# Retention and a routed expert layer on one core: the first job's second weights are loaded behind its rows, two lists are set a step apart, and the rows of zeros go out in three scatters

## The chip, the cores and the metric

The kernel runs on one core of a Trainium2 chip. The metric is the device time of one execution in microseconds (us). Several executions of the kernel before were timed, and one execution was also taken by the hardware profiler. Engines are named as the profile names them: PE (matrix multiplies; PEld is its weight load), DVE and ACT (element work), POOL (element work, and the issue of indirect transfers), SP (the issue of plain transfers).

## The reference, cut to what matters

```python
# q, k, v: (B=4, H=8, S=768, D=64)
gamma = 1.0 - 2.0 ** (-5.0 - np.arange(H))
for t in range(S):
    state = gamma * state + k[:, :, t] outer v[:, :, t]
    y[:, :, t] = (q[:, :, t] @ state) / sqrt(D)

x = y as 3072 tokens of 512 features
logits = x @ w_gate + modality_bias[modality_id]      # 8 experts
e_idx = argmax(logits);  gate_w = softmax(logits)[e_idx]
for e in range(8):
    rows = x[e_idx == e]
    out[e_idx == e] = gate_w * (relu(rows @ w1[e]) @ w2[e])   # w1: 512x1024, w2: 1024x512
```

A decayed linear attention gives one row for each of 3072 tokens. Each row then goes to one of eight experts, a two-layer network, and the result goes back to the token's place.

## The kernel before, in words

**Attention and routing.** The 3072 tokens are 24 chunks of 128. `retention` works through them, by `whole_*` functions for the first nine chunks and by `quarters` for the rest; it is a generator that yields several times a chunk. Every three chunks are a group (eight groups, numbered from 0), and `route(gr)` routes one. Its pieces are small functions on a list `todo`: `a` and `a1` find each token's expert, `b` ranks tokens and 256-row candidates (PE tiles `pc` and `rk`), `c` scatters the three chunks' rows to `x_dram`, sorted by expert (POOL, L485), and makes the one-hot `ohs` (PE tile `pk` ahead of it), and `d` writes an event list `lst` (PE tile `pt`). `wait` does nothing; it takes one place. `tick` runs the next piece: at each yield of `retention` before the first job, and at every second step of a job later. Such lists follow groups 1, 2, 4, 5 and 6. Each names two full slots of 256 rows that can be computed already; so there are ten event jobs (two for each list, tags e10, e11, e20 and so on) and two jobs from the final list. Two units of 32 rows, and a loop for what is left over, take the rest.

**A job** loads its rows (`xg0`, `xg1`, SP, L810) and its expert's weights as raw f32 (`raw1i` for w1 and `raw2i` for w2, 512 KB each, L778, or L780 where the load is skipped if the wanted expert is there already). Each raw tile is cut in a high part (`hi`, ACT, L784) and a low part (`lo`, DVE, L786). The rows are transposed on PE, eight matmuls (`flip_x`, tile `xp`, L829). Then `first_slot` computes h (L844) and `second` computes o (L859), three products each; the result is scattered to the output by POOL (L872). During a job, every third step does a piece of the next chunk of attention.

**The guess.** After group 0 the most frequent expert is guessed to be that of the first job, and `everything` loads its w1 and w2 (L778) before the list is known. When the list of group 1 is there, the job starts: its rows and then both weights again, conditionally. After that, `ahead` counts the remaining yields down from AHEAD = 6: the first two pieces of w1 are cut at 4 and 3, the rows are flipped at 2, and the job begins at 0.

**Padding.** Each expert's last slot is filled with rows of zeros: `pad_a` and `pad_b` compute, for each of eight experts, 256 row numbers (11 DVE operations), and `pad_c` issues two scatters for an expert (POOL, L545) of 128 rows each, most of whose numbers are out of range. The zeros are a tile of 128 x 514 that POOL fills at L173. The rows of the first job from the final list wait for all of them.

**What sets the order.** PE, ACT, DVE and SP run in the order in which the Python calls emit their instructions; POOL's order is set by a scheduler. A new tile in a pool's buffer waits for the readers of the old one. Attention's `kq` tiles are in a pool of four buffers, with the exception of four early ones that lie in tiles of the jobs.

## Time and profile before

| | us |
|---|---|
| median of 3 executions | 432.29 |
| their lowest and highest | 431.11, 435.65 |
| the profiled execution | 429.24 |
| span in the profile | 427.2 |
| PE busy | 403.8 (95%) |
| DVE busy | 247.5 (58%) |
| ACT busy | 207.7 (49%) |
| POOL busy | 103.1 (24%) |

A row of the timeline gives the start, the duration, the engine, the line, the operation with its output and inputs, how many instructions are merged, and in brackets how long the engine stood idle before and what ended that. PEclk is the TensorE clock that was granted, 1.00 being full speed. "issue" is a time in which the engine waited for nothing that the profile shows.

### The profile page before, as it was taken

To read this page: it belongs to the slowest core of one execution; us is meant where nothing else is said; L and a number is where in the kernel's file an instruction comes from. 1 tells how busy PE (TensorE), PEld (TensorE's weight loads), DVE (VectorE), ACT (ScalarE), POOL (GpSimd) and SP (SyncE) were. 2 spreads that over 40 slices of the span, in tenths; PEclk is the share of its full clock that TensorE was granted. 3 is DMA by queue.
4 is the path that set the end of the run, shared out by engine and by line. 5 is a ranking of instruction groups with operands and counts; after the bars stand their busy time and mean duration, and the time that the engine had idled before them with its cause. 6 is when DMAs were issued, how large, how long until landed. Compare 5 with 4: busy or idle time off the path is not lost.

```text
span 427.2 us, 12026 instructions
## 1 busy us (share of the span) xinstructions
PE 403.8 (95%) x4596; PEld 352.8 (83%) x4596; DVE 247.5 (58%) x590; ACT 207.7 (49%) x420; POOL 103.1 (24%) x130
## 2 busy tenths in 40 slices
PE   4998869999999999999999999999999999999994
PEld 3887749988968977988898998989899898967863
DVE  1775537855726674756754765768565574634700
ACT  1233346754627444655645564655465563636511
POOL 2424401233033114112510210130486100002001
PEclk9998979999999999999999999999999999999998
DMA  8999748877787955137760213762253898999001
GB/s 289 398 405 371 270 143 263 297 265 252 255 294 261 302 209 187 50 125 254 241 224 28 94 58 123 269 201 76 67 174 130 310 337 280 383 387 345 27 0 45
DMA packets 30891, 92.79 MB, mean 217 GB/s; under 512 B 5550, under 2 KB 5678, under 8 KB 30832
## 3 DMA queue, kind: packets, MB, share of 16 engines
q1 hardware_dynamic: 25360, 77.83, 52.8%
q0 software_dynamic: 5184, 13.67, 8.6%
q8 instruction: 37, 0.61, 0.6%
q10 hardware_dynamic: 288, 0.50, 0.3%
q14 instruction: 22, 0.18, 0.1%
HBM read 94.84 MB, written 17.21 MB: 262 GB/s over the span
## 4 chain that ended last, share of the span: by engine, by line
PE 54%; issue 17%; DMA 5%; DVE 3%; POOL 3%; ACT 2%; POOLq 1%; SPq 0%; ACTq 0%
PE o_e L859 20%; PE h_e L844 20%; PE x L379 4%; PE st L267 3%; PE sc L267 3%; PE y L267 2%; DVE lo_e L786 2%; PE xp_e L829 2%; ACT hi_e L784 1%; DMA kv<-in_qkv_dram 1%; POOL out_dram L872 1%; POOL x_dram L545 1%; DMA x_dram<-zer,pad_i 1%; DMA xg_e<-x_dram 1%; DMA wa_u<-in_w_dram 1%
## 5 line engine op out<-in xcount | busy, mean ns | idle before, releaser
L786 DVE TENSOR_TENSOR lo_e<-raw,hi_e 128x1024 fp32r<-128x1024 f32 x80 | 99.8, 1248 | 83.9 <-ACT hi_e L784 75.9
L844 PE MATMUL h_e<-xTh,hi_e 128*128 128x256 f32 x320 | 91.8, 287 | 0.0
L844 PE MATMUL h_e<-xTl,hi_e 128*128 128x256 f32 x320 | 90.3, 282 | 0.0
L844 PE MATMUL h_e<-xTh,lo_e 128*128 128x256 f32 x320 | 90.3, 282 | 0.0
L784 ACT CAST hi_e<-raw 128x1024 fp32r<-128x1024 f32 x80 | 83.7, 1047 | 3.9 <-DMA raw<-in_w_dram 3.9
L859 PE MATMUL o_e<-hi_e,hTh 128*128 128x512 f32 x160 | 66.3, 414 | 0.0
L859 PE MATMUL o_e<-lo_e,hTh 128*128 128x512 f32 x160 | 63.1, 395 | 0.0
L859 PE MATMUL o_e<-hi_e,hTl 128*128 128x512 f32 x160 | 63.1, 394 | 0.0
L844 PEld LDWEIGHTS h_e<-xTh,hi_e 128*128 128x128 f32 x320 | 60.7, 190 | 0.7
L844 PEld LDWEIGHTS h_e<-xTh,lo_e 128*128 128x128 f32 x320 | 60.6, 190 | 0.3
L844 PEld LDWEIGHTS h_e<-xTl,hi_e 128*128 128x128 f32 x320 | 60.7, 190 | 0.0
L1032 POOL TENSOR_TENSOR vd<-kv,cst 128x512 f32<-128x512 f32 x24 | 27.2, 1133 | 96.7 <-PE y L267 38.7
L793 ACT ACTIVATE hTh<-h_e 128x256 fp32r<-128x256 f32 x80 | 30.7, 386 | 34.0 <-PE h_e L844 29.9
L872 POOL DMA_INDIRECT out_dram<-o_e,xg_e x20 | 20.6, 1032 | 110.2 <-ACT o_e L871 90.4
L401 ACT ACTIVATE xs<-x,cst 128x64 f32<-128x64 f32 x96 | 22.2, 314 | 43.7 <-DVE lh L387 25.1
L794 DVE SCALAR_TENSOR_TENSOR hTl<-h_e,hTh 128x256 fp32r<-128x256 f32 x80 | 33.1, 419 | 16.5 <-ACT hTh L793 14.8
L485 POOL DMA_INDIRECT x_dram<-xs,pos x24 | 26.9, 1119 | 44.9 <-DVE a L212 17.2
L859 PEld LDWEIGHTS o_e<-lo_e,hTh 128*128 128x128 f32 x160 | 30.1, 188 | 7.1
L859 PEld LDWEIGHTS o_e<-hi_e,hTh 128*128 128x128 f32 x160 | 30.1, 188 | 6.1
L859 PEld LDWEIGHTS o_e<-hi_e,hTl 128*128 128x128 f32 x160 | 30.2, 189 | 5.5
L871 ACT ACTIVATE o_e<-o_e,xg_e 128x512 f32<-128x512 f32 x20 | 13.8, 690 | 40.8 <-issue 23.9
L379 PE MATMUL x<-wgt,yT 128*128 128x144 f32 x192 | 30.7, 304 | 1.8 <-issue 1.8
(193 smaller groups left out, 677.8 us busy)
## 6 DMA issues: line engine op xcount, KB each, us to landing
raw<-in_w_dram SPq DMA_DIRECT2D x104, 512.0 KB
kv<-in_qkv_dram SPq DMA_DIRECT2D x24, 512.0 KB
kq<-in_qkv_dram SPq DMA_DIRECT2D x23, 512.0 KB
xg_e<-x_dram SPq DMA_DIRECT2D x20, 257.0 KB
wa_u<-in_w_dram SPq DMA_DIRECT2D x8, 512.0 KB
wb_u<-in_w_dram SPq DMA_DIRECT2D x16, 256.0 KB
xg_s<-x_dram SPq DMA_DIRECT2D x4, 257.0 KB
x_dram<-xs,pos POOLq DMA_INDIRECT x24
```

The source lines that it names most:

```text
L267: nc.tensor.matmul(out_, l, r, start=start, stop=True, skip_group_check=True)
L379: nc.tensor.matmul(px[:, g], yT[:, 2 * u + g], wgt[:, 2 * u + g], start=(g == 0), stop=(g == 1), skip_group_check=True,)
L401: nc.scalar.activation(x[:, i], px[:, i // 2, rows(i % 2)], AF.Copy, scale=gain[:, c, 4 * u + i : 4 * u + i + 1],)
L485: ins = nc.gpsimd.indirect_dma_start(out=x_dram[:, :], out_offset=bass.IndirectOffsetOnAxis(ap=pos[:, i : i + 1], axis=0), in_=xs, in_offs ...
L784: nc.scalar.copy(hi, raws[m][i])
L786: nc.vector.tensor_tensor(lo, raws[m][i], hi.bitcast(F32), op=ALU.subtract)
L793: nc.scalar.activation(hi, src, AF.Relu)
L794: nc.vector.scalar_tensor_tensor(lo, src, 0.0, hi.bitcast(F32), op0=ALU.max, op1=ALU.subtract)
L844: nc.tensor.matmul(ph, s["w1"][f // 2][wi][:, o : o + P], s["xT"][kc // 2][a][:, kc % 2, :], start=(n == 0), stop=(n == 3 * KC - 1),)
L859: nc.tensor.matmul(po, hT[f][a][:, hh * P : (hh + 1) * P], s["w2"][f // 2][wi][:, (f % 2) * DM : (f % 2 + 1) * DM], start=(n == 0), stop=( ...
L872: ins = nc.gpsimd.indirect_dma_start(out=out[:, :], out_offset=bass.IndirectOffsetOnAxis(ap=xg.bitcast(I32)[:, DM : DM + 1], axis=0), in_= ...
L1032: ins = nc.gpsimd.tensor_tensor(vds[n], vv, by[:, n % NCH].unsqueeze(2).to_broadcast([P, H, D]), op=ALU.mult)
```

## The change

1. The guess loads w1 alone. The first job loads its w2 without a condition, behind its rows and the conditional w1.
2. AHEAD is 5, the flip stands at `ahead == 1`, and the first list's pieces are `a1, wait, b, c, d`: b, c and d come one step later. The cuts and the beginning of the job stay at their steps, since the count starts one step later.
3. The fifth group's pieces (gr 4) are `a, a1, wait, b, c, d, rows_out`, one step later from b on.
4. Both row registers of the first job are read ahead of its first row load.
5. The four `kq` buffers become slices of one tile `four`, which the padding fills with zeros for runs of eight rows (128 x 4112), and which also holds the last units' w1.
6. The padding is three scatters: two of runs of eight rows, one of single rows. Their row numbers take 26 DVE operations in place of 11, three small matmuls in place of one, and two more places on `todo` ahead of the scatters.

```diff
@@ constants @@
+RUN = 8
-AHEAD = 6
+AHEAD = 5
@@ buffers of kq @@
+    four = ld.tile([P, max(4 * QW, RUN * ROW)], F32, name="four", bufs=1)
+    fours = [four[:, i * QW : (i + 1) * QW] for i in range(4)]
+    free = [i for i in range(NN) if ("kq", i) not in lent]
+        if kind == "kq":
+            return fours[free.index(n) % 4].rearrange("p (a b) -> p a b", a=2)
@@ pad_m, pad_b, pad_c (new) @@
+        for i in range(3):
+            nc.tensor.matmul(
+                tot[:, i : i + 1], spread[:, i], ones[:, 0:1], start=True, stop=True
+            )
+        mid["zero"] = zer = four[:, : RUN * ROW].rearrange("p (r c) -> p r c", c=ROW)
+        nc.gpsimd.memset(zer, 0.0)
...
+    def pad_c(i):
+        n = RUN if i else 1
+        zer = mid["zero"].rearrange("p r c -> p (r c)")
+        ins = nc.gpsimd.indirect_dma_start(
+            out=x_dram[:, :].rearrange("(n r) c -> n (r c)", r=n),
+            out_offset=bass.IndirectOffsetOnAxis(ap=mid["pad"][:, i : i + 1], axis=0),
+            in_=zer[:, : n * ROW],
+            in_offset=None,
+            bounds_check=ZROW // n - 1,
+            oob_is_err=False,
+        )
@@ load_rows, unit, start_job @@
-            r = r() if callable(r) else r
-        wa = [ld.tile([P, QW], F32, tag="kq", name=f"wa{i}_{tag}", bufs=4) for i in range(4)]
+        wa = fours
-        s["at"] = [lambda h=h: reg(lst, at + h * n + i, EMPTY) for h in range(s["nh"])]
+        s["at"] = [reg(lst, at + h * n + i, EMPTY) for h in range(s["nh"])]
@@ route @@
-            todo.extend([a1, b, c, d])
+            todo.extend([a1, wait, b, c, d])
-            todo.extend([a, a1, b, c])
+            todo.extend([a, a1, wait, b, c])
-                todo.extend([wait, final_m, wait, final_b, pad_a, wait, pad_b, wait])
-                todo.extend([lambda e=e: pad_c(e) for e in range(NE)])
+                todo.extend([wait, final_m, wait, final_b, pad_a, wait, pad_m, wait, pad_b, wait])
+                todo.extend([lambda i=i: pad_c(i) for i in (1, 2, 0)])
@@ everything @@
                 raw(guess, 1)
-                raw(guess, 2)
                     raw(job, 1, guess)
-                    raw(job, 2, guess)
+                    raw(job, 2)
-                if ahead == 2:
+                if ahead == 1:
                     flip_x(job)
```

How this moves the instructions is shown at three places. On SP, before, this stands between the guess's last raw tile and the first job's rows (`lst_798` is the first list in memory; each read of it gives one register, `xg_e_803` and `xg_e_815` are the two halves of the rows):

```order
L778 DMA raw_109<-in_w_dram 128x1024
L111 DMA kv_739<-in_qkv_dram 128x1024
L958 TENSOR_LOAD lst_798
L958 ISA x2
L810 ISA
L810 DMA xg_e_803<-x_dram 128x514
L958 TENSOR_LOAD lst_798
L958 ISA x2
L810 ISA
L810 DMA xg_e_815<-x_dram 128x514
L958 TENSOR_LOAD lst_798
L958 ISA x2
```

And now, from the guess's last raw tile on (the tiles' numbers differ):

```order
L807 DMA raw_105<-in_w_dram 128x1024
L120 DMA kv_702<-in_qkv_dram 128x1024
L986 TENSOR_LOAD lst_810
L986 ISA x2
L986 TENSOR_LOAD lst_810
L986 ISA x2
L838 ISA
L838 DMA xg_e_835<-x_dram 128x514
L838 ISA
L838 DMA xg_e_837<-x_dram 128x514
L986 TENSOR_LOAD lst_810
L986 ISA x2
```

The four raw tiles 106 to 109 (w2) no longer stand ahead of `kv`, and both row registers are read ahead of the first row load. The w2 loads now come behind the conditional w1, which ends with `raw_105`:

```order
L809 DMA raw_105<-in_w_dram 128x1024
L807 ISA
L807 DMA raw_106<-in_w_dram 128x1024
L807 ISA
L807 DMA raw_107<-in_w_dram 128x1024
L807 ISA
L807 DMA raw_108<-in_w_dram 128x1024
L807 ISA
L807 DMA raw_109<-in_w_dram 128x1024
L120 DMA kv_867<-in_qkv_dram 128x1024
L114 DMA four<-in_qkv_dram 128x1024
```

They stand ahead of the next chunks' kv and kq (a slice of `four`), where the four conditional w2 loads stood.

On PE, before, the flip (`xp`) stands behind the last matmuls of chunk 8's y and ahead of the work on chunk 9 (`st`, `y` with input `s_9`):

```order
L319 MATMUL y_8_944<-a_773,vd_701 64x128 x4
L319 MATMUL y_8_945<-a_773,vd_701 64x128 x4
L829 MATMUL xp_e_969<-cst,xg_e_803 128x128
L829 MATMUL xp_e_969<-cst,xg_e_815 128x128
L829 MATMUL xp_e_969<-cst,xg_e_803 128x128
L829 MATMUL xp_e_969<-cst,xg_e_815 128x128
L829 MATMUL xp_e_978<-cst,xg_e_803 128x128
L829 MATMUL xp_e_978<-cst,xg_e_815 128x128
L829 MATMUL xp_e_978<-cst,xg_e_803 128x128
L829 MATMUL xp_e_978<-cst,xg_e_815 128x128
L267 MATMUL st_897<-vd_866,kv_320 64x64 x2
L267 MATMUL y_987<-kq_287,s_9_906 64x64 x2
```

And now:

```order
L276 MATMUL sc_958<-four 64x64 x2
L276 MATMUL y_957<-four,s_9_927 64x64 x2
L276 MATMUL sc_958<-four 64x64 x2
L276 MATMUL y_957<-four,s_9_927 64x64 x2
L857 MATMUL xp_e_993<-cst,xg_e_835 128x128
L857 MATMUL xp_e_993<-cst,xg_e_837 128x128
L857 MATMUL xp_e_993<-cst,xg_e_835 128x128
L857 MATMUL xp_e_993<-cst,xg_e_837 128x128
L857 MATMUL xp_e_1002<-cst,xg_e_835 128x128
L857 MATMUL xp_e_1002<-cst,xg_e_837 128x128
L857 MATMUL xp_e_1002<-cst,xg_e_835 128x128
L857 MATMUL xp_e_1002<-cst,xg_e_837 128x128
```

The flip has gone behind the first half of chunk 9's small matmuls; between `y_8` and the flip there are now 32 of them. In the same list, `pc` and `rk` of the first list's `b` have gone behind chunk 8's scores (`sc_8`, L277, 16 matmuls), `pk` behind the routing product of chunk 6 (`x`, L379), and `pt` behind chunk 7's y; on DVE the operations from `gt` to `ohs` have gone behind chunk 8's `a`.

On PE in the fifth group, before, the pieces of `b` (`pc`, `rk`) stand inside the first output half of job e20 (`o_e_2584`), behind its first 12 matmuls:

```order
L859 MATMUL o_e_2584<-hi_e_2374,hTl_2392 128x512
L859 MATMUL o_e_2584<-lo_e_2376,hTh_2391 128x512
L619 LDWEIGHTS crep
L619 MATMUL pc_2609<-ones,crep 96x1
L456 LDWEIGHTS upper
L456 MATMUL rk_2618<-oh_2541,upper 128x24
L457 LDWEIGHTS ones
L457 MATMUL rk_2618<-ebase,ones 128x24
L463 LDWEIGHTS ones
L463 MATMUL rk_2618<-cnt_95,ones 128x24
L463 LDWEIGHTS ones
L463 MATMUL rk_2618<-oh_2541,ones 128x16
```

And now:

```order
L887 MATMUL o_e_2565<-hi_e_2497,hTl_2515 128x512
L887 MATMUL o_e_2565<-lo_e_2499,hTh_2514 128x512
L648 LDWEIGHTS crep
L648 MATMUL pc_2671<-ones,crep 96x1
L465 LDWEIGHTS upper
L465 MATMUL rk_2680<-oh_2522,upper 128x24
L466 LDWEIGHTS ones
L466 MATMUL rk_2680<-ebase,ones 128x24
L472 LDWEIGHTS ones
L472 MATMUL rk_2680<-cnt_95,ones 128x24
L472 LDWEIGHTS ones
L472 MATMUL rk_2680<-oh_2522,ones 128x16
```

They stand behind the end of that half, ahead of the second half `o_e_2696`. In the same way `pk` has gone behind the first 12 matmuls of the second half, and `pt` behind its end.

More of the change, by code (lines that the diff above doesn't have):

```diff
@@ L497, in pad_a @@
     def pad_a():
-        tot = bank("tot")[:, :NE]
-        nc.tensor.matmul(tot, ones, cnt[NGRP], start=True, stop=True)
-        shape = [P, NE, 2]
-        at = cp.tile(shape, F32, name="pad_at")
-        row = cp.tile([P, 2], F32, name="pad_row")
-        nc.gpsimd.iota(
-            row, [[P, 2]], base=0, channel_multiplier=1, allow_small_or_imprecise_dtypes=True
-        )
-        num = cp.tile([P, NE], F32, name="pad_num")
-        nc.vector.tensor_copy(num, tot)
-        numi = cp.tile([P, NE], I32, name="pad_numi")
@@ L543, in pad_c @@
-    def pad_c(e):
-        for h in range(2):
-            ins = nc.gpsimd.indirect_dma_start(
-                out=x_dram[:, :],
-                out_offset=bass.IndirectOffsetOnAxis(ap=mid["pad"][:, e, h : h + 1], axis=0),
-                in_=mid["zero"],
-                in_offset=None,
-                bounds_check=ZROW - 1,
-                oob_is_err=False,
-            )
-            disjoint(ins, "x_rows")
+        spread = cp.tile([P, 3, P], BF16, name="pad_cnt")
+        for to, n in ((spread[:, 0], 16), (spread[:, 1:].rearrange("p d c -> p (d c)"), 32)):
+            nc.vector.tensor_copy(
+                to.rearrange("p (e j) -> p e j", j=n),
+                cnt[NGRP].unsqueeze(2).to_broadcast([P, NE, n]),
+            )
@@ new lines, in pad_b @@
+    def pad_b():
+        tot, base, j = mid.pop("pad")
+        num = cp.tile([P, 3], F32, name="pad_tot")
+        nc.vector.tensor_copy(num, tot)
+        left = cp.tile([P, 3], F32, name="pad_left")
+        nc.vector.tensor_scalar(left, num, -1.0, float(NT), op0=ALU.mult, op1=ALU.add)
+        lefti = cp.tile([P, 3], I32, name="pad_lefti")
+        nc.vector.tensor_copy(lefti, left)
+        ones_i = cp.tile([P, 3], I32, name="pad_ones_i")
+        nc.vector.tensor_scalar(ones_i, lefti, RUN - 1, None, op0=ALU.bitwise_and)
+        one = cp.tile([P, 3], F32, name="pad_one")
+        nc.vector.tensor_copy(one, ones_i)
+        nc.vector.tensor_scalar(lefti, lefti, SLOT - 1, None, op0=ALU.bitwise_and)
+        nc.vector.tensor_copy(left, lefti)
+        nc.vector.tensor_tensor(base, base, num, op=ALU.add)
+        nc.vector.tensor_tensor(base[:, 1:], base[:, 1:], one[:, 1:], op=ALU.add)
+        for t in (left, base):
+            if t is left:
+                nc.vector.tensor_tensor(t[:, 1:], t[:, 1:], one[:, 1:], op=ALU.subtract)
+            nc.vector.tensor_scalar(t[:, 1:], t[:, 1:], 1.0 / RUN, None, op0=ALU.mult)
+        nc.vector.tensor_copy(left[:, 0:1], one[:, 0:1])
+        nc.vector.tensor_tensor(base, base, j, op=ALU.add)
+        over = cp.tile([P, 3], F32, name="pad_over")
+        nc.vector.tensor_tensor(over, j, left, op=ALU.is_ge)
+        nc.vector.tensor_scalar(over, over, float(2 * ZROW), None, op0=ALU.mult)
+        at = mid["pad"] = cp.tile([P, 3], I32, name="pad_i")
+        nc.vector.tensor_tensor(at, over, base, op=ALU.add)
@@ L556 @@
+    def pad_c(i):
[8 more added lines that the diff above has]
+            oob_is_err=False,
+        )
+        disjoint(ins, "x_rows")
     off_c = cnd[:, 0:1]
```

52 lines of the change are left out of this document (19 added, 33 removed).

## The prediction

> **What bounds the kernel now.** I began with the page's first part and then looked for PE's idle time, since PE is nearly always busy.
>
> ```profile
> span 427.2 us, 12026 instructions
> PE 403.8 (95%) x4596; PEld 352.8 (83%) x4596; DVE 247.5 (58%) x590; ACT 207.7 (49%) x420; POOL 103.1 (24%) x130
> ```
>
> PE is idle for 427.2 − 403.8 = 23.4 us. The change removes no PE work worth counting, so it can win only what lies in these gaps, and in the slow clock that follows some of them. The timeline of PE, from the start of the first job on, has the largest group of gaps:
>
> ```profile
> start us, us, engine line op out<-in xcount [idle before <-releaser]
> 57.06 0.30 PE L829 MATMUL xp_e<-cst,xg_e 128*128 128x128 f32 x1 [1.03 <-DMA xg_e<-x_dram]
> 58.47 1.34 PE L829 MATMUL xp_e<-cst,xg_e 128*128 128x128 f32 x7 [1.11 <-DMA xg_e<-x_dram]
> 61.92 0.37 PE L267 MATMUL st<-vd,kv 64*64 64x64 f32 x2 [2.12 <-ACT s L262]
> 66.76 0.37 PE L844 MATMUL h_e<-xTh,hi_e 128*128 128x256 f32 x1
> ```
>
> PE waits 1.03 and 1.11 us for the two halves of the rows, flips them, and then waits 2.12 us for ACT's `s`; the first job's h begins at 66.76. The same place by stretches of 4 us (PE, PEld, DVE, ACT and POOL busy, granted clock, DMA share, GB/s):
>
> ```profile
> 40.00:44.00 4.00, 4.00 (x52) 3.35 (x53) 3.22 (x14) 1.86 (x7) 0.64 (x1) 0.76 1.08 278
> 44.00:48.00 4.00, 3.75 (x61) 3.22 (x59) 3.69 (x19) 0.37 (x1) 1.43 (x2) 1.00 0.96 357
> 48.00:52.00 4.00, 2.83 (x64) 2.46 (x60) 1.22 (x8) 1.81 (x7) 2.74 (x3) 1.00 0.74 289
> 52.00:56.00 4.00, 3.97 (x75) 3.31 (x72) 0.00 (x0) 0.41 (x2) 0.24 (x1) 1.00 0.22 53
> 60.00:64.00 4.00, 2.08 (x76) 2.08 (x80) 2.02 (x7) 3.32 (x10) 0.21 (x1) 0.50 0.67 245
> 64.00:68.00 4.00, 4.00 (x81) 3.78 (x75) 3.20 (x10) 2.14 (x8) 0.98 (x1) 0.78 0.97 277
> ```
>
> Two things are to be seen: the DMA engines are full until 48 us and nearly empty from 52 to 56, and PE works at half clock after the gap. What releases the first job is a chain over four engines, read from the timelines of POOL, SP and ACT:
>
> ```profile
> 46.75 1.03 POOL L485 DMA_INDIRECT x_dram<-xs,pos  x1 [2.35 <-DVE full L680]
> 49.36 0.97 POOL L485 DMA_INDIRECT x_dram<-xs,pos  x1 [0.30 <-issue]
> 30.91 4.96 SPq L778 DMA_DIRECT2D raw<-in_w_dram  x8
> 54.15 1.92 SPq L810 DMA_DIRECT2D xg_e<-x_dram  x2
> 57.07 3.09 SPq L780 DMA_DIRECT2D raw<-in_w_dram  x8
> 57.17 1.04 ACT L784 CAST hi_e<-raw 128x1024 fp32r<-128x1024 f32 x1 [3.92 <-DMA raw<-in_w_dram]
> 61.48 0.39 ACT L262 COPY s<-st 128x256 f32<-128x256 f32 x1
> ```
>
> The last scatter of group 1 starts at 49.36; the rows' load is issued 4.79 us later, when all scatters have landed (54.15); the conditional raws come 2.92 us behind it (57.07), since a row register is read between the two row loads. The first cut waits for them (57.17), and DVE's low part, chunk 9's work and ACT's `s` (61.48) follow in order, so that PE resumes 4.75 us after the cut began.
>
> The second place is the fifth group, in job e20 (PE, then DVE):
>
> ```profile
> 155.10 0.20 PE L619 MATMUL pc<-ones,crep 128*96 128x1 bf16 x1 [0.43 <-DVE crep L614]
> 165.33 0.21 PE L692 MATMUL pt<-ohs,vals 96*1 96x2 bf16 x3 [0.69 <-DVE ohs L682]
> 154.84 0.21 DVE L614 COPY crep<-cnt 128x96 bf16<-128x96 bf16 x1
> ```
>
> The third is the padding (POOL, DVE, the chain of waits, PE):
>
> ```profile
> 303.31 0.98 POOL L545 DMA_INDIRECT x_dram<-zer,pad_i  x1 [9.90 <-issue]
> 316.57 0.98 POOL L872 DMA_INDIRECT out_dram<-o_e,xg_e  x1 [0.30 <-ACT o_e L871]
> 326.51 0.98 POOL L545 DMA_INDIRECT x_dram<-zer,pad_i  x1 [0.30 <-issue]
> 327.80 0.98 POOL L872 DMA_INDIRECT out_dram<-o_e,xg_e  x1 [0.30 <-issue]
> 302.36 0.17 DVE L539 TENSOR_TENSOR pad_i<-pad_over,pad_row 128x16 int32<-128x16 f32 x1
> 305.00 1.22 DVE L786 TENSOR_TENSOR lo_e<-raw,hi_e 128x1024 fp32r<-128x1024 f32 x1
> 310.86 1.23 DVE L786 TENSOR_TENSOR lo_e<-raw,hi_e 128x1024 fp32r<-128x1024 f32 x1 [4.65 <-ACT o_e L871]
> 315.67 0.70 ACT o_e L871
> 327.80 2.92 DMA out_dram<-o_e,xg_e
> 330.83 3.56 DMA xg_e<-x_dram
> 334.44 0.98 PE L829 MATMUL xp_e<-cst,xg_e 128*128 128x128 f32 x7 [0.37 <-DMA xg_e<-x_dram]
> ```
>
> Eighteen indirect transfers follow each other on POOL from 303.31 to 328.78. The second half of the rows waits for the output scatter queued behind them, which lands 2.92 us after its start; PE loses 0.37 us.
>
> **The change part by part.** *First job, scatters.* `pc` and `rk`, and with them the row positions, go behind chunk 8's scores on PE:
>
> ```profile
> 44.26 1.16 PE L277 MATMUL sc<-kq 64*128 64x128 f32 x16
> ```
>
> The three scatters move by these 1.2 us: the last starts at 50.6. The landing is not known in the new order. The upper bound is today's 4.79 us; the lower is the 2.92 us of the output scatter at 327.80. Four raws of 512 KB are gone from the queue ahead; at the 357 GB/s of 44 to 48 us 2.1 MB is 5.9 us, so the queue is empty by about 45 rather than 51. I take 3.2 us, near the lower bound: rows issued at 53.8 (53.5 to 55.4). [...]
>
> *Registers.* Both are read while SP waits for the scatters, so row loads follow each other at once. The two row loads span 1.92 us with a read between them; without it I estimate 0.8 from the 0.62 us that one of the eight guessed loads takes to issue (4.96 / 8). So of the 3.02 us from the rows' issue to the cut (57.17 − 54.15) 1.1 go, and 1.9 stay. The cut begins at 55.7 (55.4 to 57.3), and PE resumes 4.75 us later, at 60.45 (60.15 to 62.05). PE itself is ready at about 56 today (57.06 − 1.03); that `pt` now waits for DVE's `ohs` behind `a` costs PE over a microsecond near 49, but it lies ahead of the wait for the rows and is hidden by it. If the cover went, it would cost that.
>
> *Flip.* Today it lies in the gap. Now it stands between 61.92 and 66.76, on the path. At full clock eight transposes take about 1.1 us (seven take 0.98). By the clock row, half speed lasts until 64 + 4 × (1 − 0.78) × 2 = 65.8, 3.84 us after PE resumes. So today's 4.84 us hold 1.92 + 1.0 = 2.92 us of full-speed work; with the flip 4.0, of which 1.92 again take 3.84, sum 5.9. I assume the same half clock behind the new gap, which is as long. h begins at 60.45 + 5.9 = 66.35 in place of 66.76: **−0.4 us**, by the bounds −0.7 to +1.2.
>
> *w2.* The conditional w2 loads are skipped today; now they move 2.1 MB behind the rows, from about 57 to 63, ahead of which the DMA share is 0.22 (52 to 56) and in which it is 0.67 (60 to 64). They are needed at
>
> ```profile
> 74.36 1.04 ACT L784 CAST hi_e<-raw 128x1024 fp32r<-128x1024 f32 x1
> ```
>
> so there are some 9 us of cover; the next kv and kq loads are behind them on SP by about 2 us, with the same cover or more. Nothing; if the cover went, PE would wait for the difference.
>
> *Fifth group.* The gaps of 0.43 and 0.69 go, since a step's output matmuls now stand between DVE's operation and PE's. At worst `pk` and `pt` wait for up to 0.3 us at their new places, where DVE's `ohs` again comes behind a low part. I take **−0.9 us** (−1.1 to 0). The list comes some 4 us later; what needs it are raws that lie 10 us or more ahead of their cuts.
>
> *Padding.* `pad_i` now stands behind the low part that ends at 306.2, with 17 operations of about 0.2 us (0.17 and a gap): ready at about 309.6, inside DVE's gap of 4.65 us, which hides it. The scatters of eight rows take, like all others, 0.98 us each on POOL. The last of them goes behind the output scatter that ACT releases at 316.4 (315.67 + 0.70): it is done at about 318.9 and landed, by the 2.92 − 0.98 = 1.94 us of the chain's row, at 320.8. The second row load, today at 330.83, comes by 322, so the 0.37 us go: **−0.4**. The fill of 128 x 4112 is eight times the first of these rows:
>
> ```profile
> 247.27 0.56 POOL L173 MEMSET zer<- 128x514 f32 x1
> 261.79 1.01 POOL L872 DMA_INDIRECT out_dram<-o_e,xg_e  x1 [13.80 <-ACT o_e L871]
> ```
>
> That is 4.5 us, and it fits into POOL's 13.8 us of idle time ahead of the next output scatter. The rest (one tile for four buffers, two more matmuls) lies beside PE: nothing.
>
> Sum: −0.4 − 0.9 − 0.4 = −1.7 us, so 427.5 for an execution like the profiled one (429.24). That one is 3.05 below the median of the runs shown, so I carry the difference over to the median: 432.29 − 1.7 = **430.6 us**.
>
> **The rivals.** *A, the first job gains nothing:* the scatters land as late as today and the flip is simply added: +1.2 − 0.9 − 0.4 = −0.1, so 432.2. For it: from 52 to 56 the queue is nearly empty and the rows still are not issued before 54.15.
>
> *B, slower: the scatters of eight rows are dear on POOL.* If one takes as long as eight of today's (7.9 us), the second and the two output scatters behind it end late: 310.4 + 2 × 7.9 + about 4.5 for the three others and the gaps = 330.7; with 1.9 for the landing, 0.9 to the second load and 3.56 for it, the rows are there at 337.1, 2.7 us later than today (330.83 + 3.56 = 334.4). Sum −0.4 − 0.9 + 2.7 = +1.4: 433.7. It turns the sum's sign where one takes 7.2 us. Against it: the row scatters (0.97) and the zero scatters (0.98) cost POOL the same although most of the zero rows are out of range, so the count of indices sets the time.
>
> *C, a larger gain:* with 2.1 MB fewer in the queue, the gap and the clock dip ahead of the first list go too.
>
> ```profile
> 36.00:40.00 4.00, 2.13 (x15) 1.78 (x12) 0.48 (x2) 1.51 (x6) 2.92 (x4) 0.81 1.02 389
> 38.30 0.95 PE L379 MATMUL x<-wgt,yT 128*128 128x144 f32 x3 [1.77 <-issue]
> ```
>
> That is 1.77 idle, and 4 × 0.19 + 4 × 0.24 = 1.7 of clock, the part of it before 38.3 being idle anyway; some 3 us more, sum −4.7: 427.6. Against it: the queue is still full then, since the missing four raws would have been its last. [...]
>
> *D, the change doesn't do what it says:* the guess is wrong, or something else in the first job's chain ends last; then only −1.3 remains, 431.0, inside the forecast.
>
> **How the numbers follow.** Forecast (with D) 0.58, A 0.20, B 0.10, C 0.12. A measurement of this kernel tells about 1% from no change: 4.3 us. The forecast's own bounds are −2.2 to −0.2, 430.1 to 432.1; with C below, and A and B above, and the runs' own spread (431.11 to 435.65), the range is 427.4 to 433.7. Faster by over 1% (below 428.0) is most of C and little else: 0.13. Slower by over 1% (above 436.6) needs B and a slow median: 0.05. The same: 0.82.
>
> **What would show it.** Right: the last scatter of group 1 near 50.6 and the rows' load 3 to 3.5 us behind it; the first cut near 55.7; one unbroken PE gap ending near 60.5; h at about 66.4; no gap ahead of `pc` and `pt` in the fifth group; three zero scatters of 1 us and no gap ahead of the flip near 334. Wrong: rows issued after 55, a gap ahead of the cuts of w2, zero scatters of several microseconds, or a low part on DVE pushed back by the longer arithmetic.

## The result, and the profile after

| | before | after |
|---|---|---|
| median of 6 executions, us | 433.15 | 427.35 |
| their lowest and highest | 431.11, 435.65 | 426.21, 428.57 |
| the profiled execution | 429.24 | 426.21 |
| span in the profile | 427.2 | 424.4 |

The ratio of the medians is 0.9865 (95% interval 0.9822 to 0.9908): 1.35% or 5.8 us faster, where 1.7 us were forecast. From one profiled execution to the other it is only 3.0 us. So there are two questions: where the 3.0 us lie, and why the other executions of before are slower than the profiled one, which is faster than every one of the six that were timed. Here and below, a ratio leaves out executions over 1.5% slower than the fastest of their kernel and a median doesn't, so the two can differ a little.

The first part of the page of after shows that PE lost 1.4 us of busy time (403.8 before) and 1.4 us of idle time (23.4 before, 424.4 − 402.4 = 22.0 now), and that POOL has 12 instructions fewer:

```profile
PE 402.4 (95%) x4598; PEld 352.2 (83%) x4598; DVE 250.3 (59%) x605; ACT 207.8 (49%) x420; POOL 92.9 (22%) x118
```

The starts of the jobs' first h matmul, read from PE's timelines, place the gain (us from the span's start; the column of differences is after minus before, and the last column how much of it arose since the row above):

| | before | after | difference | of it here |
|---|---|---|---|---|
| first job | 66.8 | 66.3 | −0.5 | −0.5 |
| second | 100.3 | 98.9 | −1.4 | −0.9 |
| third | 135.5 | 134.0 | −1.5 | −0.1 |
| fourth (behind the fifth list) | 169.5 | 166.7 | −2.8 | −1.3 |
| ninth (the padding is issued in it) | 315.4 | 312.8 | −2.6 | +0.2 |
| tenth | 339.4 | 336.3 | −3.1 | −0.5 |
| end of the span | 427.2 | 424.4 | −2.8 | +0.3 |

**The first job.** After's timelines of POOL, SP and ACT show the chain that releases it: the last scatter of group 1, the rows, the conditional w1, the first cut. (ACT's `s` follows at 60.23.)

```profile
48.88 0.97 POOL L494 DMA_INDIRECT x_dram<-xs,pos  x1 [0.30 <-issue]
53.87 0.88 SPq L838 DMA_DIRECT2D xg_e<-x_dram  x2
55.82 1.86 SPq L809 DMA_DIRECT2D raw<-in_w_dram  x4
55.91 1.04 ACT L813 CAST hi_e<-raw 128x1024 fp32r<-128x1024 f32 x1 [3.08 <-DMA raw<-in_w_dram]
```

PE at the same place, with the three gaps ahead of it:

```profile
36.93 0.76 PE L388 MATMUL x<-wgt,yT 128*128 128x144 f32 x4 [1.38 <-issue]
38.38 0.76 PE L388 MATMUL x<-wgt,yT 128*128 128x144 f32 x4 [0.69 <-ACT yT L334]
48.63 0.21 PE L721 MATMUL pt<-ohs,vals 96*1 96x2 bf16 x3 [1.84 <-DVE ohs L711]
60.67 0.37 PE L276 MATMUL st<-vd,kv 64*64 64x64 f32 x2 [2.91 <-ACT s L271]
62.59 1.67 PE L857 MATMUL xp_e<-cst,xg_e 128*128 128x128 f32 x8
66.27 0.38 PE L872 MATMUL h_e<-xTh,hi_e 128*128 128x256 f32 x1
```

One gap stands where there were three; PE resumes at 60.67 instead of 61.92, and then has the flip ahead of h. By stretches of 4 us (the columns as in the prediction):

```profile
36.00:40.00 4.00, 2.38 (x24) 2.02 (x24) 1.25 (x6) 1.57 (x6) 2.23 (x4) 1.00 1.05 379
40.00:44.00 4.00, 4.00 (x66) 3.64 (x64) 3.72 (x12) 1.68 (x6) 1.04 (x1) 1.00 0.44 116
44.00:48.00 4.00, 2.38 (x37) 1.74 (x37) 3.72 (x19) 0.59 (x3) 1.42 (x2) 1.00 0.18 68
48.00:52.00 4.00, 3.17 (x65) 2.86 (x66) 0.91 (x6) 1.25 (x5) 2.61 (x3) 0.77 0.50 185
52.00:56.00 4.00, 4.00 (x46) 3.61 (x44) 0.00 (x0) 0.46 (x2) 0.00 (x0) 0.50 0.29 76
```

The DMA share is 0.44 and 0.18 where it was 1.08 and 0.96: the queue runs empty several microseconds earlier, before the last scatter starts. The clock is full from 36 to 48, where it had been 0.81 and 0.76; the half clock has moved to 48 to 56, into the time in which PE would wait for the rows anyway.

**The fifth list.** PE's timeline no longer shows a gap ahead of `pc` and `pt`:

```profile
158.09 0.17 PE L648 MATMUL pc<-ones,crep 128*96 128x1 bf16 x1
166.58 0.21 PE L721 MATMUL pt<-ohs,vals 96*1 96x2 bf16 x3
```

**The padding.** Three scatters around the output scatters on POOL (the first of the three at 306.84, the last at 315.32), the rows' load on SP 10 us earlier than the second load of before (330.83), and PE's flip without a gap ahead of it:

```profile
306.84 0.98 POOL L574 DMA_INDIRECT x_dram<-four,pad_i  x1 [16.05 <-issue]
314.04 0.98 POOL L900 DMA_INDIRECT out_dram<-o_e,xg_e  x1 [3.66 <-ACT o_e L899]
315.32 1.49 POOL L574 DMA_INDIRECT x_dram<-four,pad_i  x1 [0.30 <-DMA raw<-in_w_dram]
320.86 0.96 SPq L838 DMA_DIRECT2D xg_e<-x_dram  x2
331.22 1.03 PE L857 MATMUL xp_e<-cst,xg_e 128*128 128x128 f32 x8
```

### The profile page after: what moved, and what is told of

Same layout as the page of the kernel before. It is cut to its first block, busy times and chain, and to the rows that moved or that the text cites. A ratio compares the mean times of both kernels' runs of the same rounds, so it can differ in the third digit from the quotient of the medians.

```text
span 424.4 us, 12003 instructions
## 1 busy us (share of the span) xinstructions
PE 402.4 (95%) x4598; PEld 352.2 (83%) x4598; DVE 250.3 (59%) x605; ACT 207.8 (49%) x420; POOL 92.9 (22%) x118
## 4 chain that ended last, share of the span: by engine, by line
PE 57%; issue 24%; POOL 2%; DVE 1%; DMA 1%; ACT 1%; POOLq 1%; ACTq 0%
PE h_e L872 22%; PE o_e L887 19%; PE x L388 4%; PE sc L276 3%; PE st L276 3%; PE y L276 2%; PE xp_e L857 2%; POOL out_dram L900 2%; DMA raw<-in_w_dram 1%; DVE lo_e L815 1%; ACT hi_e L813 0%; POOL out_dram L974 0%; POOL x_dram L574 0%; POOLq L914 0%; PE rk L472 0%
## 5 line engine op out<-in xcount | busy, mean ns | idle before, releaser
L1058 POOL TENSOR_TENSOR vd<-kv,cst 128x512 f32<-128x512 f32 x24 | 28.4, 1184 | 107.2 <-DMA kv<-in_qkv_dram 51.7
```

The lines of the kernel that those rows point to most:

```text
L1058: ins = nc.gpsimd.tensor_tensor(vds[n], vv, by[:, n % NCH].unsqueeze(2).to_broadcast([P, H, D]), op=ALU.mult)
```

## The experiments

The theory to begin with was that the three places have the sizes that the profiles show, and that the rest of the 5.8 us is a cost that most executions of before pay and its profiled one didn't; the rivals were that it comes from the first job, or from the padding. A further rival is that the profile and the timed executions of the first comparison came from different chips; the record doesn't say where each was taken, and no run rules this out. The runs came in four sets. The kernels of a set ran on one chip and share the executions of before there; chips differ (before: 435.1, 425.1, 429.6 and 425.0 in the four), so times are compared within a set only.

### First set: the parts alone

`b0_before_again` is the kernel before, unchanged.

> The kernel before, unchanged, profiled once more. Two theories of the 5.8 us between the medians. Clock theory: the gaps that the change removes are worth 2 to 3 us, and the rest is where the slow-clock stretches of 3.4 us fall against PE's gaps, which differs from one execution to the next; then this execution's trace shows its half-clock stretches at other places than 38.5 to 41.9 and 59 to 65.8, and its span lies anywhere from 427 to 434. Queue theory: the loads taken out of the queue are worth the rest in every execution; then this trace repeats the first one within 0.5 us up to the first job's h (66.8), and the higher median comes from elsewhere.

`p1_first_alone` has parts 1, 2 and 4 (the first job) on the kernel before:

```diff
-AHEAD = 6
+AHEAD = 5
-            r = r() if callable(r) else r
-        s["at"] = [lambda h=h: reg(lst, at + h * n + i, EMPTY) for h in range(s["nh"])]
+        s["at"] = [reg(lst, at + h * n + i, EMPTY) for h in range(s["nh"])]
-            todo.extend([a1, b, c, d])
+            todo.extend([a1, wait, b, c, d])
-                raw(guess, 2)
-                    raw(job, 2, guess)
+                    raw(job, 2)
-                if ahead == 2:
+                if ahead == 1:
```

> Parts 1, 2 and 4 alone on the kernel before (w2 behind the rows, the first list and the flip a step later, both registers read first). Clock theory: h of the first job begins 0.3 to 1 us earlier than in a trace of before with the same slow stretches, and the median falls by 0.5 to 2 us. Queue theory: the median falls by 3.5 to 4.5 us, most of the whole change.

`p2_fifth_alone` has part 3 alone:

```diff
-            todo.extend([a, a1, b, c])
+            todo.extend([a, a1, wait, b, c])
```

> Part 3 alone (the fifth list's b, c and d one step later). Both theories: the gaps ahead of pc (0.43) and pt (0.69) are gone and nothing takes their place, 1.1 us in the trace between the same two instructions; the median falls by about 1 us, less than three rounds can tell.

`p3_pads_alone` has parts 5 and 6 alone: the tile `four` and the three scatters.

> Parts 5 and 6 alone (one tile for the four buffers, three scatters of zeros). Both theories: the gap of 0.37 us ahead of the flip of the last-but-one job is gone, the first zero scatter starts near 310 and each takes about 1 us on POOL; 0.4 us. If the scatters of zeros cost more than the one gap (their traffic beside the weights' loads), the part is worth 1.5 us or more, and the trace shows it as shorter waits between 303 and 340.

Measured against before's 435.10, together with the start of the first job's h in each profile, and the time from one job's first h to the next one's at the two other places (third to fourth: the fifth list; ninth to tenth: the padding):

| | median, us | ratio (95%) | first h | third to fourth | ninth to tenth |
|---|---|---|---|---|---|
| before again | 435.39 | 1.0006 (0.9966 to 1.0046) | 66.5 | 34.0 | 29.1 |
| first job alone | 433.47 | 0.9955 (0.9915 to 0.9995) | 65.9 | 34.0 | 28.4 |
| fifth list alone | 433.30 | 0.9944 (0.9903 to 0.9985) | 67.3 | 32.8 | 28.6 |
| padding alone | 428.10 | 0.9800 (0.9756 to 0.9844) | 66.3 | 34.1 | 23.4 |

The padding alone gives 7.0 us, more than the whole change gave in the first comparison, where 0.4 had been expected of it. And the trace of before again shows what the first one hadn't: the ninth job takes 29.1 us, not 24.0, and 28.4 and 28.6 us in the two other kernels of this set that have the sixteen scatters. With three it takes 23.4. Neither theory of before again foresaw this: the loss begins at full clock (the rows below), and the first job's parts, of which the queue theory expected 3.5 to 4.5 us, give 1.6. The timed executions of before in this set fall into two groups, nine from 431.4 to 433.7 and thirteen from 435.0 to 438.7; all four of the padding alone, 427.15 to 428.87, lie below both.

The long job has two forms. In the fifth list's kernel it is a wait for the rows, from POOL and PE:

```profile
328.67 1.30 POOL L872 DMA_INDIRECT out_dram<-o_e,xg_e  x1 [0.30 <-issue]
333.65 0.33 PE L829 MATMUL xp_e<-cst,xg_e 128*128 128x128 f32 x1 [0.36 <-DMA xg_e<-x_dram]
336.86 1.75 PE L829 MATMUL xp_e<-cst,xg_e 128*128 128x128 f32 x7 [2.88 <-DMA xg_e<-x_dram]
```

The output scatter at the end of POOL's row starts at 328.67 here, 327.80 in the first profile of before, which is 0.87 us later; but it also lands in 4.70 us, at 333.37, where it was 2.92. So the load of the second half of the rows is issued at 333.48 (330.83 before). PE loses 0.36 + 2.88 us, and the granted clock behind it is 0.59:

```profile
336.00:340.00 4.00, 3.14 (x11) 2.85 (x12) 1.38 (x2) 1.94 (x3) 0.00 (x0) 0.59 1.03 416
```

The 0.37 us of the prediction were the edge of this. In before again and in the first job's kernel the rows are in time, and the time is lost earlier; by stretches of 4 us, first before again, then the first job alone, then the first profile of before, then the padding alone:

```profile
320.00:324.00 4.00, 2.26 (x13) 1.86 (x13) 1.69 (x3) 1.89 (x3) 3.35 (x3) 1.00 0.54 139
```

```profile
320.00:324.00 4.00, 2.82 (x18) 2.33 (x18) 1.67 (x3) 1.61 (x3) 3.39 (x3) 1.00 0.61 160
```

```profile
320.00:324.00 4.00, 4.00 (x36) 4.00 (x36) 2.74 (x6) 2.85 (x5) 3.09 (x4) 1.00 0.64 245
```

```profile
320.00:324.00 4.00, 4.00 (x36) 4.00 (x35) 2.61 (x5) 2.75 (x5) 0.00 (x0) 1.00 0.39 153
```

POOL is about as busy as in the first profile (3.35 and 3.39 us, 3.09 there), but PE runs 13 or 18 matmuls in 4 us instead of 36, at a granted clock of 1.00. In before again a stretch at 0.60 comes behind it; in the first job's kernel none does, and its job is still 28.4 us long, so half clock isn't what makes this form long. The waits of PE from 312 to 330 in before again name no releaser, and only 2.7 us:

```profile
PE h_e L844 <- issue: 2.7, 6, 1.0
```

The delay begins ahead of that stretch: the records of PE's matmuls for the job's o end at 315.1, and ACT takes that o only at 318.95, where the first profile has 315.67. What holds it up is not shown.

The first job alone gives 1.6 us and the fifth list 1.8 us, with intervals that barely exclude no change; the h of the first job is 0.6 us earlier and the fifth list's job 1.2 us shorter, but the rest of each median is not placed by these traces, and lies within the scatter between executions.

### Second set: the number of scatters

`a0_after_again` is the kernel after, unchanged.

> The changed kernel, unchanged, for the kernels beside it. In all traces of the old padding but the first, the job that runs beside the scatters of zeros (h from 315) takes 28.4 to 29.1 us; in the first it took 24.0, and with the new padding 23.4 to 23.5. All theories of the padding: 23.5 again, and 6 to 8 us less than the kernel before.

`e1_after_13_empty` has thirteen scatters more than after, so that there are sixteen again; every index of the added ones is out of range, so that they write nothing:

```diff
+        none = mid["none"] = cp.tile([P, 1], I32, name="pad_none")
+        nc.vector.tensor_scalar(none, base[:, 0:1], float(4 * ZROW), None, op0=ALU.add)
-    def pad_c(i):
+    def pad_c(i, empty):
...
+        for _ in range(empty):
+            ins = nc.gpsimd.indirect_dma_start(
+                out=x_dram[:, :],
+                out_offset=bass.IndirectOffsetOnAxis(ap=mid["none"], axis=0),
+                in_=zer[:, :ROW],
...
-                todo.extend([lambda i=i: pad_c(i) for i in (1, 2, 0)])
+                todo.extend([lambda i=i, n=n: pad_c(i, n) for i, n in ((1, 4), (2, 4), (0, 5))])
```

> The changed kernel with 13 more scatters between and behind the three of zeros, whose row numbers are all out of range, so that POOL issues 16 as before but no more bytes move. Count theory (sixteen issues of 128 numbers each hold up the output scatters behind them and slow PE beside them, whatever they move): the job goes back to 28 to 29 us and the gain of the padding, 5 us or more, is gone. Row theory (the zeros written as separate rows of 2 KB are what hurts): the job stays at 23.5 us and the time within 1 us of the changed kernel.

`e2_pads_six` is the kernel before with the scatters of three experts only; the ten that are left out are out of range altogether:

```diff
-                todo.extend([lambda e=e: pad_c(e) for e in range(NE)])
+                todo.extend([lambda e=e: pad_c(e) for e in (0, 3, 5)])
```

> The kernel before with the scatters of zeros of experts 0, 3 and 5 alone, which for these inputs are the ones that have rows to fill: 6 scatters in place of 16, the same rows of 2 KB written. It leaves out 10 scatters whose numbers are all out of range. Count theory: the job beside them takes about 23.5 us, and the time falls by 5 us or more against the kernel before. Row theory: the job still takes 28 to 29 us and the time is that of the kernel before within 1.5 us.

`e3_no_first` is the kernel after without parts 1, 2 and 4.

> The changed kernel without parts 1, 2 and 4 (the first job as before), with the fifth list and the padding changed. If the first job's parts are worth what the traces show, 0 to 0.6 us with the slow clock falling here or there, it is slower than the changed kernel by 0 to 1 us; if they are worth the 1.6 us that the difference of medians gave for them alone, by 1 to 2.5 us.

| | median, us | ratio to before's 425.12 (95%) | ninth to tenth h |
|---|---|---|---|
| after again | 422.69 | 0.9939 (0.9911 to 0.9967) | 23.5 |
| after and 13 empty scatters | 429.87 | 1.0100 (1.0076 to 1.0125) | 31.7 |
| before with six scatters | 424.71 | 0.9980 (0.9960 to 1.0000) | 23.4 |
| after without the first job's parts | 423.22 | 0.9955 (0.9935 to 0.9975) | 23.4 |

On this chip the change brings 2.4 us, near the 1.7 of the prediction and not the 6 to 8 expected here, and taking ten of the old padding's scatters away brings only 0.4, where the count theory expected 5. So before seems not to have the long job here in most executions; it wasn't profiled on this chip. But thirteen empty scatters cost 7.2 us (429.87 − 422.69), as the count theory expected and the row theory didn't; the job is even longer than forecast (31.7 for 28 to 29). They move no bytes; they end late, and the rows wait for the last of them. POOL, SP and PE:

```profile
327.60 0.98 POOL L586 DMA_INDIRECT x_dram<-four,pad_none  x1 [0.30 <-issue]
329.88 0.96 SPq L850 DMA_DIRECT2D xg_e<-x_dram  x2
333.14 0.48 PE L869 MATMUL xp_e<-cst,xg_e 128*128 128x128 f32 x1 [4.95 <-DMA xg_e<-x_dram]
334.44 1.76 PE L869 MATMUL xp_e<-cst,xg_e 128*128 128x128 f32 x7 [0.82 <-DMA xg_e<-x_dram]
```

The last empty scatter starts at 327.60 and has landed 2.1 us later, and the rows are issued then. The output scatter that POOL issues next, at 328.89, holds nothing up: it lands at 333.74, after both row loads were issued. PE's two gaps are 5.77 us, and half clock follows:

```profile
332.00:336.00 4.00, 2.03 (x9) 1.74 (x10) 0.00 (x0) 0.59 (x1) 0.00 (x0) 0.50 1.01 369
```

The rows are issued about when they are in the first profile of before (329.88 and 330.51, there 328.72 and 330.83), but PE reaches this place 5.8 us earlier (the ninth job begins at 309.6, there at 315.4), so the wait is longer than the old padding's. So thirteen issues that move nothing, ahead of a load that waits for the last of them, are enough for the late form (31.7 us from the ninth to the tenth h, where after has 23.5); it needs no more bytes. No run brings back the other form, the slowed PE, with empty scatters.

Without the first job's parts the time is 0.5 us higher than after again, and the first h comes at 66.5, not 65.5. The rows are where the two differ, first without those parts, then after again:

```profile
46.71 0.97 POOL L494 DMA_INDIRECT x_dram<-xs,pos  x1 [0.30 <-issue]
53.62 1.93 SPq L839 DMA_DIRECT2D xg_e<-x_dram  x2
```

```profile
47.51 0.98 POOL L494 DMA_INDIRECT x_dram<-xs,pos  x1 [0.31 <-issue]
51.93 0.88 SPq L838 DMA_DIRECT2D xg_e<-x_dram  x2
```

With w2 in the queue ahead (DMA share 0.83 from 48 to 52) the rows come 6.91 us behind the last scatter's start; without it (0.31) 4.42. The scatters start 0.8 us later, and the rows are issued 1.7 us earlier.

### Third set: is it the scatters alone, and what does w2 do

`b1_before` is the kernel before, unchanged.

> The kernel before once more, to have its trace beside the next three on one chip. So far the medians of the kernel before were 433, 435 and, in the last comparison, 425 us, and the job beside the padding took 24.0, 29.1 us in its two traces. Edge theory: the rows of the last-but-one job arrive within 0.4 us of when PE wants them, so a little more delay in POOL's queue of 18 transfers costs a wait and a stretch of half clock; this trace then shows either about 24 us and a time near 425 to 430, or 27 to 30 us and a time above 431, nothing between.

`e4_pads_six_again` repeats the six scatters of the second set, on another chip.

> Six scatters of zeros in place of 16, the same rows written. Edge theory: the job beside the padding takes 23.4 us whatever the kernel before does here; so the gain is about 0.5 us where the kernel before is at 425, and 5 us or more where it is at 433 or above. If rows of 2 KB are what hurts, it stays as slow as the kernel before.

`e5_pads_alone_again` repeats the padding alone of the first set.

> Parts 5 and 6 alone. Edge theory: as the kernel with six scatters, within 1 us. If the runs of eight rows are worth something of their own, 2 us or more less than that.

`e6_w2_alone` has part 1 alone on the kernel before. It is to show how far behind the start of the last scatter the rows' load is issued, for which the prediction has 3 to 3.5 us with the queue emptied:

```diff
-                raw(guess, 2)
-                    raw(job, 2, guess)
+                    raw(job, 2)
```

> Part 1 alone: the guess loads w1 only, w2 comes behind the rows. [...] Rival: the landing is the scatters' own (4.99 us with the changed kernel, whose queue was nearly empty); then the load comes 4.6 to 5.2 us behind, and h moves by less than 0.5 us apart from where the slow clock falls.

| | median, us | ratio to before's 429.56 (95%) | first h | ninth to tenth |
|---|---|---|---|---|
| before | 429.43 | 0.9989 (0.9949 to 1.0028) | 66.4 | 23.9 |
| six scatters | 428.09 | 0.9947 (0.9910 to 0.9985) | 66.6 | 23.4 |
| padding alone | 428.29 | 0.9950 (0.9914 to 0.9986) | 67.0 | 23.4 |
| w2 alone | 429.62 | 0.9960 (0.9912 to 1.0007) | 66.6 | 26.1 |

The ninth job of w2 alone, which has the sixteen scatters, takes 26.1 us. That is between the two lengths that were expected of before here, with "nothing between". Its rows are in time; PE runs 27 matmuls from 320 to 324, so it is a weaker case of the slowed PE.

Six scatters of single rows do as much as the three with runs, within the intervals: the tile `four`, the runs of eight rows and the longer arithmetic add nothing that can be seen. (Six were run on this chip and the second set's only, not on the first set's, where the old padding costs most.) The padding alone gives less here than in the first set, 1.3 us by the medians against 7.0, as the old padding costs less here: the profile of before has the short ninth job (23.9), PE waiting 0.20 us for the second half of the rows:

```profile
333.08 0.98 PE L829 MATMUL xp_e<-cst,xg_e 128*128 128x128 f32 x7 [0.20 <-DMA xg_e<-x_dram]
```

With w2 alone the guess's four raws are out of the queue, and yet the rows are issued 4.13 us behind the start of the last scatter (49.29 to 53.42, POOL and SP):

```profile
49.29 0.97 POOL L485 DMA_INDIRECT x_dram<-xs,pos  x1 [0.30 <-issue]
53.42 1.47 SPq L810 DMA_DIRECT2D xg_e<-x_dram  x2
```

That lies between the prediction's 3 to 3.5 us for the emptied queue and the 4.6 to 5.2 of a landing that is the scatters' own, and meets neither. In before on this chip the scatter starts at 49.31 too and the rows come at 53.90, so part 1 makes them 0.5 us earlier. PE resumes 0.85 us earlier (60.81 for 61.66), but its half clock falls later, onto the way to h (from 64 to 68 the granted clock is 0.50, 0.85 in before), and h comes at 66.6 for 66.4. So what part 1 alone gained at the first job was lost to the clock in this pair of executions; one trace each doesn't tell more.

### Fourth set: empty scatters for which nobody waits, and the flip

`e7_empty_early` adds the same number of empty scatters to after, with an index tile that needs no arithmetic, so that POOL's scheduler puts them early: they are issued from 249.7 to 270.3, some 50 us ahead of the padding:

```diff
+    def pad_empty(count):
+        if "out" not in mid:
+            mid["out"] = cp.tile([P, 1], I32, name="pad_out")
+            nc.gpsimd.memset(mid["out"], 2 * ZROW)
+        for _ in range(count):
+            ins = nc.gpsimd.indirect_dma_start(
+                out=x_dram[:, :],
+                out_offset=bass.IndirectOffsetOnAxis(ap=mid["out"], axis=0),
...
+                todo[-3:] = [lambda f=f, n=n: (f(), pad_empty(n)) for f, n in zip(todo[-3:], (4, 4, 5))]
```

> The changed kernel with 13 scatters whose numbers are all out of range, issued by POOL near 253 to 270, some 50 us ahead of the padding, where no load of rows waits for them and only two output scatters are queued among them. If the issues themselves slow PE (stutter without a wait in the traces of the kernel before from 319 to 326), PE's matmuls between 253 and 270 show gaps without a releaser of 1 us or more, and the time is 1 to 3 us above the changed kernel. If it takes somebody who waits for the end of POOL's queue, PE shows no such gap there and the time is within 0.7 us of the changed kernel.

`a1_after` is the kernel after, unchanged.

> The changed kernel, unchanged, on the same chip: the reference for the other two. The spread of its times stays within 2.5 us; the kernel before has some executions 5 us above its others.

`e8_flip_early` is after with the flip back at its old step:

```diff
-                if ahead == 1:
+                if ahead == 2:
                     flip_x(job)
```

> The changed kernel with the flip one step earlier, between y of chunk 8 and the work on chunk 9, where the kernel before had it; the list, w2, registers, the fifth list and the padding stay changed. By the prediction's step on the flip (1.1 us on the path behind the wait for the rows, hidden ahead of it) PE flips inside its wait, resumes chunk 9 at the same time and begins h 1 to 1.3 us earlier than the changed kernel. Rival: the flip, in front of chunk 9, waits for the second half of the rows longer than ACT's s is late, so h begins no earlier (within 0.3 us).

| | median, us | ratio to before's 425.02 (95%) | first h |
|---|---|---|---|
| after and 13 empty, early | 422.01 | 0.9930 (0.9906 to 0.9954) | 65.6 |
| after | 422.74 | 0.9941 (0.9921 to 0.9960) | 65.1 |
| after, flip at its old step | 420.71 | 0.9906 (0.9885 to 0.9927) | 64.3 |

Early, thirteen empty scatters cost nothing (422.01 us, after 422.74). POOL is busy with them (3.17 of 4 us) and PE isn't slowed (4.00 of 4 and 25 matmuls, 26 in after on the same chip):

```profile
258.00:262.00 4.00, 4.00 (x25) 3.48 (x24) 2.10 (x5) 1.64 (x4) 3.17 (x3) 1.00 0.71 214
```

So a POOL busy with scatters in a row didn't by itself slow PE here. What did it in before again stays open: on this chip before is at 425 and may not have that slow form at all, so the run speaks only against the general claim. The time is 0.73 us below after's, at the edge of the 0.7 that was expected to hold.

The flip at its old step is 2.0 us faster than after by the medians (420.71 against 422.74; highest 421.88, where after's is 423.06) and 1.5 by the ratios, and faster than both kernels of the case on this chip. PE, first with the old step, then after on the same chip:

```profile
55.38 0.30 PE L857 MATMUL xp_e<-cst,xg_e 128*128 128x128 f32 x1 [2.13 <-DMA xg_e<-x_dram]
59.42 0.37 PE L276 MATMUL st<-vd,kv 64*64 64x64 f32 x2 [1.96 <-ACT s L271]
64.35 0.37 PE L872 MATMUL h_e<-xTh,hi_e 128*128 128x256 f32 x1
```

```profile
58.37 0.37 PE L276 MATMUL st<-vd,kv 64*64 64x64 f32 x2 [4.10 <-ACT s L271]
60.28 1.97 PE L857 MATMUL xp_e<-cst,xg_e 128*128 128x128 f32 x8
65.15 0.37 PE L872 MATMUL h_e<-xTh,hi_e 128*128 128x256 f32 x1
```

With the flip inside the gap, h comes 4.93 us after PE resumes; with the flip behind it, 6.78 us. The moved flip costs 1.85 us of path at half clock (its eight matmuls take 1.97 us; at full clock, at 331.22 in the profile of after, they take 1.03). Of that 0.8 us show in the first h, since PE resumes 1.05 us later with the old step. That is not the flip's doing: the rows were already issued 1.04 us later in that execution (52.62 for 51.58), ahead of the moved instructions. The expectation, that PE resumes at the same time and h comes 1 to 1.3 us earlier, was met in its direction; the rest of the 1.5 to 2.0 us isn't placed by one trace each.

## Why the prediction was right or wrong

**Scatters earlier: the time right, by two errors.** The last start was to be 50.6 and was 48.88: the half clock of 38 to 42, which I had left in place, fell elsewhere. The landing was to take 3.2 us, near its lower bound, and took 4.99, though the DMA share was 0.18 and then 0.50. So the rows came at 53.87, forecast 53.8, by luck. The step that failed is the choice of the bound. In the eight traces whose queue was emptied, the rows come 4.13 to 4.99 us behind the last scatter's start, never 3.2. That an emptied queue helps is right, but it is worth much only where the scatters start early (4.42 us for 6.91 with starts at 47.51 and 46.71, 4.13 for 4.59 with starts at 49.29 and 49.31): in the nine traces with w2 in the queue the rows are issued between 53.45 and 54.15, whether the last scatter starts at 46.71 or at 49.42, which makes 4.5 to 6.9 us. At the 49.36 of the first profile the queue was nearly done (DMA share 0.74 from 48 to 52, 0.22 behind it), and 4.79 already lay within the 4.13 to 4.99 of the emptied queue. No run shows the landing of 3.2 us that the sum uses, or one of 2.92 for these scatters, and what their landing waits for besides the loads ahead isn't shown. Rival A was right about the landing in this execution, and wrong about the time, since the scatters started earlier.

**Registers: right.** 1.9 us from the rows' issue to the first cut were forecast, 2.04 measured (53.87 to 55.91); PE resumed at 60.67 (60.45), h began at 66.27 (66.35).

**Flip: right.** The forecast was 5.9 us from PE's resuming to h, with 1.1 us of full-speed work added by the flip; after took 5.60. The direct comparison gives 1.85 us at half clock, which is 0.9 us of full-speed work. That the change would be faster without this part was in the working (the flip was the only plus in the first job's sum) and wasn't said.

**w2 and `pt`: right.** No gap at the cuts of w2; the wait of `pt` is 1.84 us at 48.63 and is followed by the rows' gap, as forecast.

**Fifth list: right.** −0.9 was forecast, −1.2 to −1.3 measured against most traces of the old list; against the third set's before, whose two gaps were smaller (0.58 in all), only some −0.5. No new wait ahead of `pk` or `pt` there.

**Padding: the step that failed.** Fill: 4.5 us estimated, measured

```profile
249.15 3.53 POOL L537 MEMSET four<- 128x4112 f32 x1 [4.46 <-PE y L276]
305.89 0.16 DVE L569 TENSOR_TENSOR pad_i<-pad_over,pad_base 128x3 int32<-128x3 f32 x1
```

and hidden; the arithmetic was done at 306.05, earlier than the 309.6 forecast; the three scatters cost POOL 0.98, 0.98 and 1.49 us, so rival B was wrong. (The count of indices, by which I argued against it, sets little of this time: the two output scatters of 32 rows take 0.88 us in before.) Up to there the path is as predicted. The rows at 320.86 for 320.8 are luck: ACT released the output scatter earlier (its o ended at 313.77, not 316.4), the last scatter was done at 316.81, not 318.9, and the rows came 4.05 us behind that, not 1.94. This cost nothing, since PE wanted them at 331.22. What was mis-sized is the term itself: I priced it at the 0.37 us of one execution, −0.4, and it was −0.5 in an execution of that kind and −5.0 to −5.7 in the three profiles of the first set that have sixteen scatters (ninth to tenth job: 28.4 to 29.1 against 23.4). The first profile had two signs of it: the rows arrived 0.37 us late behind eighteen transfers in a row, so that any delay of those went to the path at full price; and the profiled execution was faster than every timed one. I did notice the second, and carried its 3.05 us over to the median unchanged, which says that the change doesn't touch what makes the other executions slower. The first set shows that it does there. Of the six profiles with the old padding, the ninth job is short in two (24.0 and 23.9), the rows are late in one (28.6), and PE is slowed in three (29.1, 28.4, 26.1). How often each form occurs isn't told by one profile for each kernel. For the late rows thirteen more scatters ahead of them, all empty, are shown to be enough (waits of 4.95 and 0.82 us); why PE is slowed stays open; shown is only that it isn't seen in the profiles with three or six scatters.

**Rival C: half right.** Of the two parts of its gain, the clock dip from 36 to 44 is gone in after, the idle time (1.38 + 0.69 for 1.77) isn't. But the dip isn't tied to the change: before in the third set has the same gap and no dip,

```profile
38.13 1.49 PE L379 MATMUL x<-wgt,yT 128*128 128x144 f32 x8 [1.76 <-issue]
40.00:44.00 4.00, 2.75 (x52) 2.28 (x48) 3.69 (x12) 1.80 (x7) 1.04 (x1) 1.00 1.08 238
```

with its granted clock at 1.00. A gap of 1.77 us was followed by a dip in one execution (granted clock 0.81 from 36 to 40 and 0.76 from 40 to 44), and one of 1.76 us by none in another (1.00 in both). What decides between the two isn't shown.

**Not explained:** 0.9 us of the profiles' difference lie between the first and the second job's h (33.5 us before, 32.6 after). It follows no part: the first job alone still has 33.6, and before with six scatters, which has the old first job, has 32.8.

**The sum.** The forecast's upper bound of −0.2 doesn't follow from its own terms: +1.2, 0 and −0.4 make +0.8, and with the fifth list's −0.9 they make −0.1. On the two chips where before ran at 425, the change gave 2.4 and 2.3 us, near the sum of 1.7. In the first comparison it gave 5.8 us, 427.35, just below the range's low end of 427.4. That the padding made the difference there is inferred from the first set, in which it alone gave 7.0; the parts weren't run beside the first comparison, and the whole change wasn't run on the chips of the first and third sets. No run shows the 3.05 us that the prediction carried over to hold for the kernel after: its profiled execution is 1.14 us below its median.

## What to carry to other kernels

Compare the profiled execution with the spread of the timed ones before pricing a term by it: where it lies outside, the others pay a cost that this trace doesn't show, and a stage where a wanted transfer arrives within a few tenths of a microsecond behind a long row of others (here 0.37 us, behind eighteen) is the first place to look. Count issues of indirect transfers, not bytes: an empty one cost POOL as much as a full one (0.98 us each), and thirteen of them cost the kernel 7.2 us where a load of rows waited for them and nothing where none did, as far as these runs show. And when a change has several parts, ask which of them has only a plus in the sum: here undoing that one (the flip's new step) gave another 1.5 to 2.0 us.

## What the runs showed of the hardware that was not expected

- An indirect scatter of 128 indices occupied POOL for 0.98 us in most cases, whether an index stood for 2 KB, for 16 KB or was out of range; some took 1.1 to 2.0 us, with the old padding and with the new. Thirteen empty ones for whose end a load of rows waited made the kernel 7.2 us slower; 50 us earlier, where nothing waited for them, the time was no higher (422.01 against 422.74).
- PE ran 13 matmuls in the 4 us from 320 to 324, where it ran 36 in the first profile of before (18 and 27 in two other profiles), at a granted clock of 1.00 and with no releaser in the profile, beside a row of sixteen scatters; no transfer of instructions lies in these 4 us of the three profiles. It was seen in three profiles with sixteen scatters and in none with three or six. The cause is open.
- The loads that wait for the three scatters of rows were issued 4.1 to 5.0 us after the last scatter's start where the queue ahead had been emptied, and 4.5 to 6.9 us after it where four loads of 512 KB more stood ahead (6.91 for 4.42 in one pair on one chip). The single output scatter of the prediction landed in 2.92 us, in another profile in 4.70, and an empty one in 2.1.
